# A gated mixer kernel: the front part in a written order, and sines taken once per matrix

## The chip, the cores and the metric

The kernel runs on one core of a Trainium2 chip. The metric is the device time of one execution in microseconds (us); the median of several runs counts. Engines are named as in the profile: PE multiplies matrices, DVE is the vector engine, ACT the scalar engine (activations and copies), POOL is GpSimd, and SP issues most of the loads. A DMA can also be issued from the queues of ACT and POOL.

## The reference

Everything is in bf16, with S = 2048 rows of D = 640 and F = 1536. From one input x (`A_q`) two branches are made and mixed by a gate:

```python
g = sigmoid((x * gate_w).sum(-1))
# branch A: a short convolution, then a long one by FFT
k_shift = sum over t<4 of shift(k, t) * shift_k[:, t]
kv = k_shift * v
y  = irfft(rfft(pad(kv)) * rfft(pad(ssm_k)))[:S] + kv * ssm_D
a  = x * y
# branch B: a mixer over shifted rows, then an MLP
h  = gelu(layernorm(x) @ w1)          # four column groups, shifted by 1, -1, 2, -2 rows
x1 = x + shifted(h) @ w2
b  = x1 + gelu(layernorm(x1) @ w3) @ w4
out = g * a + (1 - g) * b
```

## The kernel before

The 2048 rows are laid out as 128 partitions by 16 units `u` (`N2`), and four units make a chunk; `Q` holds x, one tile for each chunk.

**Branch B.** `norm_stats` (DVE, with `ve` and `rs` on POOL at L178 and L180) and `norm_apply` normalise a chunk: DVE writes `xn` (L308), PE transposes it (L315), ACT copies it to `XNT` (L90). `first_product` (PE L349) multiplies by w1 in three groups of columns: first the group of five matmuls whose left side is `W1E` (gathered columns of w1), then two groups of ten. ACT's gelus (L342) write the results to their shifted places in `GS`, those of the first group by way of `u4` and copies on POOL (L359). `second_product` (L427) multiplies a unit by w2 and DVE adds it to `Q` (L430). `third_product` (L441) and `fourth_product` (L454) are the MLP; they need `W3` and `W4`.

**Branch A.** The long convolution is a two-step Fourier transform by matrices. `filter_transpose` (L295) turns a loaded tile `HN` of the filter; DVE and ACT copy it to `HTA` and `HTB`. `step1` (L275, with ACT's copy to `AR` and a DMA to `SH` or `SX` in memory) does the first step, of the filter (`filt`, 32 rows of two matmuls) and of the convolved input. `short_conv` is eleven DVE instructions for each chunk (L413 to L418) and uses `CJ`, four copies on POOL from the loaded `CJR` (L388). `spectrum` does the second step with the matrix `M2`, multiplies, and goes back with `G1` and `G2`; `y_group` finishes.

**The matrices.** `F1`, `F1T`, `M2`, `G1` and `G2` are sines made on the chip. In `gen_step2`, POOL makes integer phases (`iota`, L244, L252, L256), DVE wraps them (L212), and ACT takes the sine (L215). `M2`, `G1` and `G2` consist of four blocks each, of which a partition needs one and holds zeros in the others. `masked_sines` takes the sine of 1024 phases four times for each matrix, with a scale and a bias per partition that are zero where the block is to be zero: twelve sines of 128x1024.

**Order.** The program is traced in the order in which it is written, and a scheduler then orders each engine's queue by that order and by when it expects operands; `tc.issue_after(x)` puts a block behind instruction x on its engine. `merge(a, b, ratio)` interleaves two generators by the costs that they yield. Tiles with one tag share a fixed number of buffers: `XNT` and `CJR` share two ("xnt"), all of PSUM's `pst` and `psw` tiles share two ("pm"), `GEN` (phases), `HTA`, `W3`, `W4` and others share three ("w"), and eleven serve `KT`, `VT`, `CJ`, `AR` and most others ("b5").

The core of the written order of the front is

```python
X0 = norm_apply(tiles_of(c4[0]), st0, "a")
...
filter_transpose(0)
st1 = norm_stats(tiles_of(c4[1]))
next(gen)
run(first_product(0, X0))
X1 = norm_apply(tiles_of(c4[1]), st1, "a")
filter_transpose(1)
```

and so on for chunks 2 and 3. `conv_front` then interleaves the convolution with `filt` and the mixer, and loads W4 (`load_w4`, on ACT's queue) behind the 32nd row of `filt`.

Of the kernel before, what the change touches and what calls it, by code (L numbers as in the profile page):

```python
# [10 lines left out]
ALU = mybir.AluOpType  # L11
# [6 lines left out]
def kernel(  # L18
# [68 lines left out]
    def evac(eng, o, i, scale=None):  # L87
        if eng == "a":
            if scale is None:
                nc.scalar.copy(out=o, in_=i)  # L90
            else:
                nc.scalar.activation(out=o, in_=i, func=ACT.Copy, scale=scale)  # L92
        else:
            assert scale is None
            nc.vector.tensor_copy(out=o, in_=i)
# [17 lines left out]
    def load_h(dt):  # L113
# [4 lines left out]
    load_q(0)  # L118
    W12 = weights("W12", [P, 2, DT, D])
# [3 lines left out]
    load_q(1)  # L123
    load_h(0)
    load_q(2)
    load_h(1)
# [3 lines left out]
    nc.scalar.copy(out=W1E.rearrange("p k (g r) -> p k g r", r=R),  # L130
                   in_=W1N.rearrange("p k (g c) -> p k g c", c=CG)[:, :, :, P:CG])
# [10 lines left out]

    IDB = consts.tile([P, P], BF16, name="IDB")
# [58 lines left out]
    with tc.issue_after(last_f.ins):  # L202
        st0 = norm_stats(tiles_of(range(4)))


# [5 lines left out]
    def masked_sines(dst, jj, ms, inner):  # L211
        nc.vector.tensor_scalar(out=jj, in0=jj, scalar1=TU - 1, scalar2=None, op0=ALU.bitwise_and)  # L212
        jv = jj.rearrange("p (o m n) -> p m o n", o=2, n=16)
        for j in range(4):
            nc.scalar.activation(out=dst[:, :, :, j, :] if inner else dst[:, :, j, :, :], in_=jv, func=ACT.Sin,  # L215
                                 bias=ms[:, 1, j:j + 1], scale=ms[:, 0, j:j + 1])

    midp = pbits(120, 0.125, 0, "midp")
    basep = pbits(3, 16, 1, "basep")
    basei = pbits(15, 512, 1, "basei")  # L220
    klf = pbits(3, 1, 0, "klf")
    kli = pbits(48, 0.0625, 0, "kli")
    offp = [pbits(4, -512, 6144 + 2048 * ro, f"offp{ro}") for ro in range(2)]
    offi = [pbits(64, -64, 6144 - 2048 * o, f"offi{o}") for o in range(2)]
    nc.vector.scalar_tensor_tensor(out=basei[:], in0=kli[:], scalar=16.0, in1=basei[:], op0=ALU.mult, op1=ALU.add)
# [3 lines left out]
    masks = []  # L229
    for name, kl in (("f", klf), ("i", kli)):  # L230
        ms = consts.tile([P, 2, 4], F32, name="ms" + name)
        for a, amp in ((0, 2 * PI_ / TU), (1, -PI_)):
            for j in range(4):
                nc.vector.tensor_scalar(out=ms[:, a, j:j + 1], in0=kl[:], scalar1=float(j), scalar2=amp,
                                                     op0=ALU.is_equal, op1=ALU.mult)
# [532 lines left out]
```

## Time and profile before

| what | value |
|---|---|
| median of 3 runs | 304.11 us (302.92 to 304.94) |
| profiled execution: time, span | 305.71 us, 303.9 us |
| PE busy, matmuls | 247.5 us, 1559 |
| DVE busy | 194.2 us |
| ACT busy | 189.0 us |
| POOL busy | 45.4 us |
| granted PE clock, mean | 0.955 |

The span runs from the first to the last instruction of the core; the execution's own time is a little longer. Busy times are sums over instructions; an engine's idle time costs nothing unless the end waits for it, so the waits and the order of the instructions have to be read beside the shares. In the views, `L123` is a line of the kernel, `xN` a number of instructions, and `A <- B` says that A waited for B.

### The profile page before, as it was taken

Reading aid. Unit: us, or ns where it says so; the run is one execution under the profiler, and the core shown is the slowest. Engines: PE = TensorE matmul, PEld = TensorE weight load, DVE = VectorE, ACT = ScalarE, POOL = GpSimd, SP = SyncE. Lnnn points to the kernel's source line nnn. Section 1 sums busy time; section 2 is a strip of 40 time slices with the busy share of each in tenths; the row PEclk is TensorE's granted clock in tenths of the full one; section 3 lists DMA queues with packets and bytes.
Section 4 is the critical chain, followed back from the end, with each engine's and each line's share of the span. In section 5 each row is a group of like instructions: output and inputs, shape, how many; then the busy total and the mean of one; then the engine's idle time right before and its main releaser. Section 6 shows DMA issues by size and latency. Waiting matters only on the chain.

```text
span 303.9 us, 4266 instructions
## 1 busy us (share of the span) xinstructions
PE 247.5 (81%) x1559; PEld 150.7 (50%) x1572; DVE 194.2 (64%) x411; ACT 189.0 (62%) x264; POOL 45.4 (15%) x79
## 2 busy tenths in 40 slices
PE   0257289389979965999999678999988997799994
PEld 0252255146545522676457455665545764445673
DVE  8781852407729869898918878996443465502982
ACT  1329975445885763743775436659789878646740
POOL 8734351620600300000000330000000000000000
PEclk9999679689999979899999999999999999799999
DMA  7991097002242599522556798696786654278741
GB/s 230 380 319 64 0 365 328 1 2 87 86 175 86 191 323 349 175 88 86 177 171 216 240 345 238 217 279 197 244 280 188 199 168 135 89 263 341 283 171 65
DMA packets 28087, 59.59 MB, mean 196 GB/s; under 512 B 2051, under 2 KB 19203, under 8 KB 28066
## 3 DMA queue, kind: packets, MB, share of 16 engines
q1 hardware_dynamic: 13042, 38.18, 38.2%
q10 hardware_dynamic: 14224, 17.70, 15.8%
q0 software_dynamic: 800, 3.44, 3.3%
q8 instruction: 12, 0.20, 0.3%
q14 instruction: 9, 0.07, 0.1%
HBM read 35.71 MB, written 18.35 MB: 178 GB/s over the span
## 4 chain that ended last, share of the span: by engine, by line
PE 58%; DMA 15%; ACT 12%; DVE 5%; POOL 4%; issue 2%; SPq 1%; ACTq 0%; POOLq 0%
PE psw L454 15%; PE psw L441 14%; PE psw L427 6%; DMA BX<-SX 5%; PE ps L275 5%; PE psz L517 5%; ACT XNT L90 4%; PE psw L349 4%; DMA HN<-in_A_ssm_k_dram 4%; DMA SH<-AR 4%; PE psy L578 3%; DMA CJR<-in_A_shift_k_dram 2%; PE psx L501 2%; PE psh L488 2%; DVE st L175 2%
## 5 line engine op out<-in xcount | busy, mean ns | idle before, releaser
L454 PE MATMUL psw<-W,G 128*128 128x320 bf16 x384 | 60.9, 299 | 2.4 <-ACT XNT L90 2.4
L90 ACT CAST AR<-ps 128x640 bf16<-128x640 f32 x64 | 41.6, 701 | 28.3 <-PE ps L275 24.3
L441 PE MATMUL psw<-XNT,W 128*128 128x512 bf16 x231 | 58.3, 387 | 0.8 <-ACT G L342 0.5
L454 PEld LDWEIGHTS <-G 128*128 128x128 bf16 x384 | 37.5, 98 | 17.5 <-issue 2.9
L506 DVE TENSOR_TENSOR XPB<-XPB,HS 128x640 bf16<-128x640 bf16 x64 | 28.3, 486 | 18.3 <-ACT XPB L90 18.3
L441 PEld LDWEIGHTS <-W 128*128 128x128 bf16 x240 | 23.7, 99 | 24.1 <-issue 2.0
L92 ACT ACTIVATE HS<-psh 128x640 bf16<-128x640 f32 x32 | 22.6, 713 | 18.4 <-PE psh L488 18.4
L342 ACT ACTIVATE G<-psw 128x1024 bf16<-128x1024 f32 x24 | 24.7, 1031 | 11.8 <-PE psw L441 11.7
L430 DVE TENSOR_TENSOR Q<-psw,Q 128x640 bf16<-128x640 f32 x16 | 12.9, 811 | 26.9 <-PE psw L427 26.9
L175 DVE BATCH_NORM_STATS2 st<-Q 128x6 f32<-128x320 bf16 x64 | 27.7, 469 | 0.5 <-DMA Q<-in_A_q_dram 0.3
L517 PE MATMUL psz<-XPB,G 128*128 128x320 bf16 x128 | 23.9, 310 | 4.9 <-DVE XPB L506 1.6
L427 PE MATMUL psw<-W,GS 128*128 128x320 bf16 x160 | 24.7, 299 | 3.3 <-ACT XNT L90 2.3
L349 PE MATMUL psw<-XNT,W 128*128 128x512 bf16 x80 | 23.5, 453 | 4.6 <-ACT u L342 4.6
L90 ACT CAST XPB<-psx 128x640 bf16<-128x640 f32 x32 | 22.3, 696 | 7.6 <-PE psx L501 7.4
L90 ACT COPY XNT<-pst 128x2048 bf16<-128x2048 bf16 (+1 forms) x16 | 19.1, 1241 | 12.2 <-PE pst L315 9.2
L308 DVE TENSOR_SCALAR xn<-Q,mv,rs 128x640 bf16<-128x640 bf16 x32 | 15.2, 520 | 15.6 <-PE pst L315 9.5
L295 PE MATMUL psh<-IDB,HN 128*128 128x128 bf16 x80 | 8.4, 278 | 18.4 <-DMA HN<-in_A_ssm_k_dram 14.8
L275 PEld LDWEIGHTS <-F 128*128 128x128 bf16 x128 | 12.5, 100 | 16.9 <-issue 8.3
L427 PEld LDWEIGHTS <-GS 128*128 128x128 bf16 x160 | 15.6, 98 | 10.0 <-issue 3.9
L178 POOL TENSOR_SCALAR ve<-mv 128x4 f32<-128x4 f32 x8 | 3.0, 370 | 111.6 <-DVE mv L176 111.6
L517 PEld LDWEIGHTS <-G 128*128 128x128 bf16 x128 | 12.6, 100 | 13.8 <-issue 5.7
L416 DVE TENSOR_TENSOR acc<-acc,tmp 128x2560 bf16<-128x2560 bf16 x12 | 17.9, 1488 | 0.3
(109 smaller groups left out, 359.8 us busy)
## 6 DMA issues: line engine op xcount, KB each, us to landing
SH<-AR ACTq DMA_DIRECT2D x8, 640.0 KB, 3.1
SX<-AR ACTq DMA_DIRECT2D x8, 640.0 KB, 3.3
BH<-SH SPq DMA_DIRECT2D x8, 640.0 KB, 4.2
HS<-HS SPq DMA_DIRECT2D x32, 160.0 KB, 2.9
BX<-SX SPq DMA_DIRECT2D x8, 640.0 KB, 5.5
SZ<-ZG ACTq DMA_DIRECT2D x8, 640.0 KB, 3.2
ZT<-SZ SPq DMA_DIRECT2D x8, 640.0 KB, 5.7
HN<-in_A_ssm_k_dram SPq DMA_DIRECT2D x5, 512.0 KB, 10.3
```

Source lines behind the costliest of these rows:

```text
L90: nc.scalar.copy(out=o, in_=i)
L92: nc.scalar.activation(out=o, in_=i, func=ACT.Copy, scale=scale)
L175: nc.vector.bn_stats(out=st[:, h, :], in_=src[i][:, h * HD:(h + 1) * HD])
L275: nc.tensor.matmul(ps[:, comp, 0:HD], lhsT=F1[:, comp, :], rhs=src[:, c0:c0 + HD], start=True, stop=True)
L342: nc.scalar.activation(out=o, in_=i, func=ACT.Gelu_apprx_tanh)
L349: nc.tensor.matmul(ps[:, j, :], lhsT=w1_cols(dt, nt), rhs=XNT[:, dt, :], start=(dt == 0), stop=(dt == DT - 1))
L416: nc.vector.tensor_tensor(out=acc[:], in0=acc[:], in1=tmp[:], op=ALU.add)
L427: nc.tensor.matmul(ps[:, h, 0:HD], lhsT=GS[:, nt, u, :], rhs=W2P[:, nt, h * HD:(h + 1) * HD], start=(nt == 0), stop=(nt == DT - 1))
L441: nc.tensor.matmul(ps[:, j, :], lhsT=W3[:, dt, (f + j) * P:(f + j + 1) * P], rhs=XNT[:, dt, :], start=(dt == 0), stop=(dt == DT - 1))
L454: nc.tensor.matmul(ps[:, h, 0:HD], lhsT=G[ft // 4][:, ft % 4, i * P:(i + 1) * P], rhs=W4[0][:, ft, h * HD:(h + 1) * HD], start=(ft == 0), ...
L506: nc.vector.tensor_tensor(out=xp[:, 1 + a, :], in0=xp[:, 0, :], in1=HS[t // 2][:, a, t % 2, :], op=ALU.mult)
L517: mm = nc.tensor.matmul(pz[:, h, 0:HD], lhsT=gm[:, t].rearrange("p a b c -> p (a b c)"), rhs=XP[t][:, 1 + a, h * HD:(h + 1) * HD], start=( ...
```

## The change

- Everything from the making of `IDB` to the end of the fourth `first_product` stands between `front.__enter__()` and `front.__exit__()`: PE, DVE, ACT and POOL run it in the order in which it is written. SP's queue isn't in that list.
- The loads of x's chunks are put ahead of the filter's: Q0, Q1, W1, Q2, HN0, Q3. W2, the second filter tile, the halo and the first K and V follow.
- The phases are mapped by six ACT instructions (`affine`) from the iotas; one DVE instruction makes the product `m1`. One sine for each matrix is written to block 3; `masked_blocks` later fills the four blocks from it under 0/1 masks, by DVE and ACT in turn, one for each step of the convolution of chunks 1 to 3.
- `W1E` is gathered by DVE (`gather_w1`) instead of ACT.
- Within `first_product(c)`, the next chunk's `norm_apply` and the statistics of the one after it are written between the second and the third group.
- `CJR`'s load and its split into `CJ` are apart. Two steps of the first convolution, and the whole of `second_product` for the first four units, lie in the front; none of `filt` does, and `conv_front` takes five rows of it for each remaining step of the first convolution instead of three.

```diff
     load_q(0)
+    load_q(1)
...
     nc.sync.dma_start(out=W1N, in_=B_w1.rearrange("(kt p) n -> p kt n", p=P))
-    load_q(1)
+    load_q(2)
     load_h(0)
-    load_q(2)
-    load_h(1)
+    load_q(3)
...
     W1E = edge("W1E")[:].rearrange("p (k n) -> p k n", n=P)
-    nc.scalar.copy(out=W1E.rearrange("p k (g r) -> p k g r", r=R),
-                   in_=W1N.rearrange("p k (g c) -> p k g c", c=CG)[:, :, :, P:CG])
+
+    def gather_w1():
+        nc.vector.tensor_copy(out=W1E.rearrange("p k (g r) -> p k g r", r=R),
+                              in_=W1N.rearrange("p k (g c) -> p k g c", c=CG)[:, :, :, P:CG])
...
+    ET = mybir.EngineType
+    front = tc.manual_schedule(engines={ET.PE, ET.DVE, ET.Activation, ET.Pool})
+    front.__enter__()
...
-    with tc.issue_after(last_f.ins):
-        st0 = norm_stats(tiles_of(range(4)))
...
-    def masked_sines(dst, jj, ms, inner):
-        nc.vector.tensor_scalar(out=jj, in0=jj, scalar1=TU - 1, scalar2=None, op0=ALU.bitwise_and)
-        jv = jj.rearrange("p (o m n) -> p m o n", o=2, n=16)
-        for j in range(4):
-            nc.scalar.activation(out=dst[:, :, :, j, :] if inner else dst[:, :, j, :, :], in_=jv, func=ACT.Sin,
-                                 bias=ms[:, 1, j:j + 1], scale=ms[:, 0, j:j + 1])
...
+    GA, GB, GC = GENW[:, 0, :], GENW[:, 1, :], GENW[:, 2, :]
+    icf, ick, icn, m1 = GA[:, 0:512], GA[:, 512:1024], GB[:, 0:512], GB[:, 512:1024].bitcast(F32)
...
     midp = pbits(120, 0.125, 0, "midp")
     basep = pbits(3, 16, 1, "basep")
...
-    masks = []
+    basei = pbits(15, 512, 1, "basei")
+    kli = pbits(48, 0.0625, 0, "kli")
+    nc.vector.scalar_tensor_tensor(out=basei[:], in0=kli[:], scalar=16.0, in1=basei[:], op0=ALU.mult, op1=ALU.add)
+    offi = [pbits(64, -64, 6144 - 2048 * o, f"offi{o}") for o in range(2)]
+    off2 = consts.tile([P, 1], F32, name="off2")
+    nc.vector.memset(off2[:], 6144.0)
...
+    def affine(o, i, scale, bias):
+        nc.scalar.activation(out=o, in_=i, func=ACT.Identity, scale=scale, bias=bias)
+
+    def wrap(jj):
+        nc.vector.tensor_scalar(out=jj, in0=jj, scalar1=TU - 1, scalar2=None, op0=ALU.bitwise_and)
+
+    def block(dst, inner, j):
+        return dst[:, :, :, j, :] if inner else dst[:, :, j, :, :]
+
+    def sines(dst, jj, inner):
+        nc.scalar.activation(out=block(dst, inner, 3), in_=jj.rearrange("p (o m n) -> p m o n", o=2, n=16),
+                             func=ACT.Sin, bias=NPI[:], scale=2 * PI_ / TU)
+
+    for ro in range(2):
+        affine(GC[:, 512 * ro:512 * ro + 512], icf, midp[:], offp[ro][:])
+    st0 = norm_stats(tiles_of(range(4)))
+    nc.vector.scalar_tensor_tensor(out=m1, in0=ick, scalar=basei[:], in1=icn, op0=ALU.add, op1=ALU.mult)
+    wrap(GC)
+    for o in range(2):
+        affine(GA[:, 512 * o:512 * o + 512], m1, 1.0, offi[o][:])
+    sines(M2, GC, True)
+    for o in range(2):
+        affine(GC[:, 512 * o:512 * o + 512], m1, 1.0, (0.0, off2[:])[o])
+    klf = pbits(3, 1, 0, "klf")
+    MK = []
...
+        mk = consts.tile([P, 4], F32, name="mk" + name)
+        MK.append(mk)
...
+    def masks():
+        for mk, kl in zip(MK, (klf, kli)):
...
-                nc.vector.tensor_scalar(out=ms[:, a, j:j + 1], in0=kl[:], scalar1=float(j), scalar2=amp,
...
-    def gen_step2():
-        GA, GB, GC = GENW[:, 0, :], GENW[:, 1, :], GENW[:, 2, :]
...
-        for ro in range(2):
-            nc.gpsimd.tensor_scalar(out=GC[:, 512 * ro:512 * ro + 512], in0=icf, scalar1=midp[:],
-                                    scalar2=offp[ro][:], op0=ALU.mult, op1=ALU.add)
-        masked_sines(M2, GC, masks[0], True)
-        yield 0.0
...
-        nc.gpsimd.tensor_scalar(out=m1, in0=ick, scalar1=basei[:], scalar2=None, op0=ALU.add)
-        nc.vector.tensor_tensor(out=m1, in0=m1, in1=icn, op=ALU.mult)
-        for (dst, jj, offs) in ((G1, GA, (offi[0][:], offi[1][:])), (G2, GC, (0.0, 6144.0))):
-            for o in range(2):
-                nc.gpsimd.tensor_scalar(out=jj[:, 512 * o:512 * o + 512], in0=m1, scalar1=offs[o], scalar2=None,
-                                        op0=ALU.add)
-            masked_sines(dst, jj, masks[1], False)
-            yield 0.0
+                nc.vector.tensor_scalar(out=mk[:, j:j + 1], in0=kl[:], scalar1=float(j), scalar2=None,
...
+                                        op0=ALU.is_equal)
+
+    def masked_blocks():
+        n = 0
+        for dst, mk, inner in ((M2, MK[0], True), (G1, MK[1], False), (G2, MK[1], False)):
+            for j in range(4):
+                if n % 2:
+                    with tc.issue_after(held["a"].ins):
+                        nc.scalar.activation(out=block(dst, inner, j), in_=block(dst, inner, 3), func=ACT.Copy,
+                                             scale=mk[:, j:j + 1])
+                else:
+                    with tc.issue_after(held["v"].ins):
+                        nc.vector.tensor_scalar(out=block(dst, inner, j), in0=block(dst, inner, 3),
+                                                scalar1=mk[:, j:j + 1], scalar2=None, op0=ALU.mult)
+                n += 1
+                yield 0.0
...
+        held["v"] = evac("v", HTA[0][:, :, dt * P:(dt + 1) * P], pst[:, 0:12, :])
+        held["a"] = evac("a", HT[3][:, :, dt * P:(dt + 1) * P], pst[:, 12:16, :])
...
-    def load_cj():
+    def load_cjr():
         cjr = main.tile([P, D, 4], BF16, name="CJR", tag="xnt", bufs=2)
         nc.gpsimd.dma_start(out=cjr[:], in_=A_shift_k.partition_broadcast(P))
+        return cjr
+
+    def split_cj(cjr):
         cj = big("CJ")
         for j in range(4):
             nc.gpsimd.tensor_copy(out=cj[:, j, :], in_=cjr[:, :, j])
...
     def load_halo(t):
+        nc.gpsimd.memset(t[0:1, :, :], 0.0)
         nc.sync.dma_start(out=t[1:113, :, :], in_=kv_[0:112, N2 - 3:N2, :])
...
+        blocks = masked_blocks()
         for g in range(NG):
             if 1 < g + 1 < NG:
                 load_kv(g + 1)
-            for c_ in short_conv(g):
+            for c_ in (short_conv(g) if g else conv0):
                 yield c_
-                for _ in range(3):
+                for _ in range(3 if g else 5):
                     next(rows, None)
+                if g > 0:
+                    next(blocks, None)
             if g == 0:
                 rows = chain(rows, step1(xrows(0), SX, 0))
             else:
                 run(rows)
                 if g < NG - 1:
                     rows = step1(xrows(g), SX, g)
+        run(blocks)
...
-    gen = gen_step2()
     X0 = norm_apply(tiles_of(c4[0]), st0, "a")
-    next(gen)
+    gather_w1()
+    wrap(GA)
+    wrap(GC)
+    sines(G1, GA, False)
+    sines(G2, GC, False)
     gs_edges()
+    st1 = norm_stats(tiles_of(c4[1]))
+    load_w2()
+    load_h(1)
     KHALO = big("KHALO", [P, 3, D])
-    nc.gpsimd.memset(KHALO[0:1, :, :], 0.0)
-    next(gen)
-    load_w2()
+    load_halo(KHALO)
+    load_kv(0)
     load_h(2)
-    load_q(3)
-    filter_transpose(0)
-    st1 = norm_stats(tiles_of(c4[1]))
-    next(gen)
-    run(first_product(0, X0))
+    first = first_product(0, X0)
+    next(first)
+    next(first)
+    masks()
     X1 = norm_apply(tiles_of(c4[1]), st1, "a")
-    filter_transpose(1)
+    st2 = norm_stats(tiles_of(c4[2]))
+    run(first)
     DROW = row("DROW")
     nc.gpsimd.dma_start(out=DROW[0:1, :], in_=A_ssm_D.rearrange("(a d) -> a d", a=1))
-    CJ = load_cj()
+    CJR = load_cjr()
+    filter_transpose(0)
     load_h(3)
-    load_halo(KHALO)
-    load_kv(0)
+    first = first_product(1, X1)
+    next(first)
+    next(first)
+    X2 = norm_apply(tiles_of(c4[2]), st2, "a")
+    st3 = norm_stats(tiles_of(c4[3]))
+    run(first)
+    filter_transpose(1)
     load_h(4)
-    st2 = norm_stats(tiles_of(c4[2]))
-    run(first_product(1, X1))
-    filter_transpose(2)
-    X2 = norm_apply(tiles_of(c4[2]), st2, "a")
-    load_kv(1)
     W3 = weights("W3", [P, DT, Fh])
     nc.sync.dma_start(out=W3[:], in_=B_w3.rearrange("(kt p) f -> p kt f", p=P))
+    load_kv(1)
+    CJ = split_cj(CJR)
+    second = second_product(US[0])
+    next(second)
+    next(second)
+    first = first_product(2, X2)
+    next(first)
+    next(first)
+    X3 = norm_apply(tiles_of(c4[3]), st3, "a")
+    run(second)
+    run(first)
+    sy0 = norm_stats(tiles_of(US[0]))
     nc.gpsimd.dma_start(out=GWB[:], in_=gate_w.partition_broadcast(P))
-    st3 = norm_stats(tiles_of(c4[3]))
+    conv0 = short_conv(0)
+    filter_transpose(2)
+    next(conv0)
     filter_transpose(3)
-    run(first_product(2, X2))
+    first = first_product(3, X3)
+    next(first)
+    next(first)
+    next(conv0)
     filter_transpose(4)
-    X3 = norm_apply(tiles_of(c4[3]), st3, "a")
+    run(first)
+    front.__exit__(None, None, None)
     rows = chain(filt(), load_w4())
-    merge(second_product(US[0]), rows, 0.4)
-    sy0 = norm_stats(tiles_of(US[0]))
-    merge(first_product(3, X3), rows, 0.4)
     Y0 = norm_apply(tiles_of(US[0]), sy0, "a")
```

## The prediction

> **What bounds the kernel now.** I read the page first (engine shares, the 40 slices), then the table of stretches, then the waits of the front alone, then the timeline of its instructions.
>
> The page, its engine line and the slice row of PE:
>
> ```profile
> PE 247.5 (81%) x1559; PEld 150.7 (50%) x1572; DVE 194.2 (64%) x411; ACT 189.0 (62%) x264; POOL 45.4 (15%) x79
> ...
> PE   0257289389979965999999678999988997799994
> ```
>
> A slice is 7.6 us. PE idles 56.4 us of the span, and most of that in the first nine slices; behind them it is 85 to 90% busy. So the kernel is a badly filled front and a PE-bound rest. The table of stretches (columns: PE, PEld, DVE, ACT, POOL busy; clock; DMA share; GB/s) says it in numbers:
>
> ```profile
> 0.00:82.30 82.30, 51.10 (x321) 30.56 (x326) 45.00 (x147) 48.22 (x64) 37.76 (x69) 0.90 0.48 172
> 82.30:303.90 221.60, 196.35 (x1240) 120.13 (x1247) 149.16 (x266) 140.79 (x200) 7.67 (x11) 0.98 0.61 205
> 82.30:107.80 25.50, 21.89 (x139) 12.81 (x139) 17.79 (x29) 17.89 (x27) 2.90 (x3) 1.00 0.44 147
> ```
>
> 82.3 us is where the last of the four `first_product` calls ends on PE, which is also where the written order of the new front ends. PE idles 31.2 us before it and 25.2 us behind it. The waits of the stretch 0 to 66 us name the holes:
>
> ```profile
> ...
> PE psh L295 <- DMA HN<-in_A_ssm_k_dram: 14.8, 2, 13.1
> ...
> ACT XNT L90 <- PE pst L315: 8.1, 1, 8.1
> ...
> PE psw L349 <- ACT XNT L90: 6.2, 2, 4.4
> ...
> PE psw L349 <- ACT u L342: 4.6, 1, 4.6
> ...
> ACT XNT L90 <- POOL CJ L388: 3.1, 1, 3.1
> ```
>
> First, PE's queue holds the filter's transposes (L295) ahead of x's, and waits until 13.07 and 16.69 us for the filter to land, though x's `xn` had been ready since 11.9; so x's first `XNT` starts at 20.69. Second, `u`'s gelu is stuck behind the sines, in this timeline:
>
> ```profile
> 22.93 4.64 ACT L215 ACTIVATE M<-GEN,msf 128x1024 bf16<-128x1024 int32 x4
> ...
> 32.46 4.65 ACT L215 ACTIVATE G<-GEN,msi 128x1024 bf16<-128x1024 int32 x4
> ...
> 52.60 3.05 POOL L388 COPY CJ<-CJR 128x640 bf16<-128x640 bf16 x4 [4.13 <-DMA CJR<-in_A_shift_k_dram]
> ...
> 55.67 2.35 ACT L90 COPY XNT<-pst 128x2048 bf16<-128x2048 bf16 x2 [3.07 <-POOL CJ L388]
> ```
>
> ACT is full from 22.9 to 37.1 with twelve sines (13.9 us), and PE, but for one filter transpose, stands from 29 until the gelus start at 38.4. Third, the last two rows: `CJR` shares the two buffers of `XNT`, so chunk 2's `XNT` waits until POOL has copied `CJ`, and PE stands 4.36 us behind it.
>
> **The change, worked along the path.** Each step is the later of what it waits for, plus durations from rows of before.
>
> *Statistics.* On DVE some 20 one-column instructions now stand ahead of the first `bn_stats`. Such rows lie 0.06 apart when independent and take 0.14 each when each needs the last: 1.2 to 2.8 us. They are written in dependent pairs, so 2.8: statistics start at 3.5 + 2.8 = 6.3 (before 3.8), take four times 0.87 to 9.8, then `ve`, `rs` 1.4 to 11.2. The phase product (a 128x512 row of 0.69) and one wrap (0.70) lie under `rs`. The four `xn` (0.45 each) run 11.4 to 13.2, begun 2.0 later than before.
>
> *Phases and sines.* Six affine maps leave POOL (rows of 0.8 to 1.6) for ACT. No row is an integer map on ACT; the nearest are the 128x512 copies at 0.61 and half a sine at 0.62, and the full 128x1024 sine row of 1.24 is the upper end. At 0.62 the first four and M2's sine (1.16) end before x's transposes do, and the last two maps lie under those transposes: nothing on the path. At 1.24 the path is 2.0 later. Two more sines follow `XNT`. Twelve sines become three: 10.4 us of ACT gone.
>
> *Chunk 0.* With x first, PE transposes from 11.9 to 13.8 (the wait for the filter is gone), ACT copies `XNT` 1.88 + 0.5 to 16.6 against 23.0 before. W1 now lands behind Q1, by the 11.3 us at which before had both; the gather (0.44 to 0.72, now on DVE) ends at 13.7. Fifteen matmuls follow, 0.43 cold and 0.22 warm, to 21.9; the sines and one table load (1.28) end at 20.3, so `u` hardly waits. Chunk 1's statistics and `xn` are done by 21.8 (its `ve` stands behind 1.8 us of edge memsets on POOL, long done; the 1.69 us KHALO memset now stands ahead of `u`'s POOL copies, which are read 20 us later). Transposes 1.3, `XNT` 1.88, and, since PSUM's two "pm" buffers hold the transposes, the last ten matmuls start only then, at 24.9: chunk 0 ends at 27.1 (before 42.9).
>
> *The stall that stays.* The filter's 16 transposes (1.06) and fifteen matmuls of chunk 1 bring PE to 31.4, chunk 2's transposes to 32.7. Its `XNT` needs a buffer. Chunk 1's is still read by ten matmuls written behind, which need the PSUM that this `XNT` frees; so only `CJR`'s is left. `CJR` can be loaded from 27.5 (x's first `XNT` free, behind DROW's issue on POOL), and lands, by before's 7.3, at 35.5; no other row of that transfer exists, the bounds are 2.0 (DROW's small one) and 14.1 (the slowest VT load). On POOL `split_cj` stands behind chunk 3's `ve`, `rs`, done at 35.9. So it runs 35.9 to 38.9, `XNT` to 40.9, and PE idles 8.2 us where before it idled 4.4. Slow landing costs up to 6.4 more; a fast one gains nothing.
>
> Behind its 4.36 us gap before's matmuls run 0.43 apart for 5 us (57.6 to 62.7) until they fall to 0.22; the new gap is charged the same way below.
>
> The Trainium skill speaks against this transfer's place ("SBUF — State Buffer", Summary: rules for kernel authors): descriptors for a load on POOL's queue are starved while DVE runs in its fast modes, and no run here shows it. If chunk 2's `xn` (1.8) held the transfer back for as long, `split_cj` would start 1.4 later and the sum be 1.4 worse.
>
> *From 40.9.* Ten matmuls 4.05 (warming), filter 1.06, two units of `second_product` 2.72, fifteen matmuls 3.24, transposes 1.33, wait for `XNT` 1.75, two units 2.72, ten matmuls 2.16, filter 2 x 1.06, fifteen 3.24, filter 1.06, ten 2.16: 27.6, so 68.5. Where the slow clock lasts longer the same sum gives 70.0. I take **69.3**.
>
> *The ledger at that point.* Before stands there at 82.3, but its PE has already done 4.9 us of the filter's `step1` (L275) and ACT twelve of its evacuations; the new front has done none. PE's lead is 82.3 - 4.9 - 69.3 = **8.1 us**.
>
> *What the rest pays.* ACT now owes 12 x 0.70 = 8.4 us of evacuations, and six masked copies at 1.03 to 1.24 (the 128x1024 rows), of which about half early, 3.1. In the stretch 82.3 to 107.8 ACT was busy 17.9 of 25.5; it becomes 17.9 + 8.4 + 3.1 = 29.4, while PE's 21.9 + 4.9 at before's rate of 86% would need 31.2. ACT would have to be 94% busy. If its waits vanish because its queue is full: no loss. If it keeps its old 70%: 42.0, a loss of 10.8. I take a third, **3.6**, since PE has ten microseconds of `second_product` ready to bring forward. On DVE six masked copies (0.43 by the `xn` row to 0.95 by the HTA row) cost 2.6 to 5.7 and two steps of the first convolution (1.33, 0.90, 0.81, 0.82, 1.48) moved into the front save 5.3: nought, under PE.
>
> The skill speaks against the masked copies on ACT ("ScalarE: Activation LUTs", Rules for kernel authors: multiplications belong on VectorE, up to three times faster in bf16); no row here has that copy on both engines. With all twelve on DVE that loss would be a third of 37.6 less 31.2, and the sum 1.5 better.
>
> Loads: SP keeps its own order; HN0, W2 and the filter land by 15 to 26 us and are first read at 27 and 45; KV0 is read at 63. W3 needs the buffer that the sines free, now at 19 instead of 37, and is read after 80. GWB's load moves behind POOL's last `rs` of the front and is read in the spectrum. All free.
>
> **Sum.** 303.9 - 8.1 + 3.6 = 299.4 of span, that is 4.5 less. The profiled execution took 305.71, 1.6 above the runs' median of 304.11, with 1.8 outside the span; I take the difference from the median: **299.6**. A measurement of this kernel tells about 1% from no change.
>
> **Rivals.**
> *(a) The stall goes too* (chunk 2's `XNT` finds a buffer without `CJ`): PE saves the 8.2, the front ends at 61.1, the lead is 16.3: 303.9 - 16.3 + 3.6 = 291.2. For it: only which buffer is given; against it: the row of before in which exactly this `XNT` waits for exactly this copy. Chance 0.14.
> *(b) ACT becomes the bound behind the front* (slower). W4's load is issued on ACT's queue behind the 32nd row of the filter. From 69.3 ACT must do `XNT` 2.4, 32 rows 22.4, masks 3.1, gelus 6.2: 34.1 us, or 48.7 at its 70%, so W4 lands (11.1) at 114.5 or 129. PE reaches `fourth_product` after 1.3 + 9.5 + 5.4 + 13.0 = 29.2 at 87%, at 102.9; with 10.8 brought forward, 113.7. The wait is 0.8 to 15.3; from 8.1 on the kernel is slower, and at the top it takes 303.9 - 8.1 + 15.3 = 311.1 (311.3 for the median). For it: all the filter's evacuations now come at once; against it: ACT has idle time in every later slice. Chance 0.25.
> *(c) The gain is lost to contention*: `CJR` lands late (6.4) and the ACT loss stays: 303.9 - 8.1 + 3.6 + 6.4 = 305.8, or 302.6 with half of it; no measurable change. For it: at 28 to 36 us the loads of chunk 3's filter rows, W3 and the second K and V may be under way; against it: `rs` holds `split_cj` as long as before's 7.3 would. Chance 0.17.
> *(d) The sines aren't saved*: the profile would show twelve Sin rows; the diff leaves three, so I give it nothing.
>
> **How the numbers follow.** The forecast, 295 to 301, has 0.44; with (a) faster has 0.58, within 1% 0.17 from (c), slower 0.25. The range runs from 290, just under (a), to 310, just under the top of (b); the forecast's own range is 294 to 305.
>
> **What would show it.** Right: `XNT` of chunk 0 at 14 to 17 us; three large Sin rows; chunk 2's `XNT` waiting for `CJ` at about 39; `first_product`'s last row (before L349) at 68 to 71; VT's first product near 80 instead of 107.8; ACT over 90% for 25 us behind it. Wrong: the front ending beyond 76, or PE waiting for W4, or no wait for `CJ`.

## The result, and the profile after

The changed kernel took 315.0 us in the median of four runs (312.9 to 317.1), the kernel before 303.7 in the same comparison: ratio 1.037, 95% interval 1.028 to 1.046. It is slower, where 299.6 had been forecast. The profiled execution took 313.56 us with a span of 311.8, so its span is 7.9 longer than that of before; the median is 11.3 longer. Ratios here and below are to the kernel before on the same chip, and leave disturbed executions out (the profiled one of cjr_own is such a one), so they can differ a little from the quotient of two medians.

The page of the changed kernel, PE's busy share and slices:

```profile
PE 246.6 (79%) x1572; PEld 148.1 (48%) x1572; DVE 198.5 (64%) x411; ACT 186.7 (60%) x265; POOL 38.1 (12%) x72
...
PE   0266729795986972899999883999998997599994
...
PEclk9997969999996998699999997899999999999999
```

PE idles 65.2 us of the span, 8.8 more than before. New holes stand behind the front: the thirteenth slice (94 to 101 us) and above all the sixteenth (117 to 125). The granted clock is low there, or in the slice that follows.

The table of stretches (PE, PEld, DVE, ACT, POOL busy; clock; DMA share; GB/s), and then the waits from 73 to 140 us:

```profile
0.00:73.00 73.00, 43.61 (x304) 25.73 (x304) 48.12 (x140) 32.34 (x46) 30.07 (x59) 0.93 0.52 176
...
73.00:100.00 27.00, 19.93 (x124) 11.31 (x121) 22.04 (x40) 21.91 (x32) 3.10 (x6) 0.92 0.43 147
...
119.00:126.00 7.00, 0.55 (x3) 0.22 (x3) 0.00 (x0) 2.93 (x3) 0.00 (x0) 0.77 1.05 380
```

```profile
DVE acc L438 <- DMA SH<-AR: 17.2, 1, 17.2
...
PE psw L479 <- DMA W<-in_B_w_dram: 6.4, 1, 6.4
...
PE ps L295 <- ACT AR L90: 6.3, 16, 2.4
DVE tmp L438 <- ACT AR L90: 3.7, 1, 3.7
ACT AR L90 <- DVE tmp L438: 2.8, 1, 2.8
```

(In the changed kernel L295 is `step1`, L370 `first_product`, L438 to L443 `short_conv`, L479 `fourth_product`.) The front now ends at 73, with 29.4 us of PE idle in it. From 119 to 126 PE works 0.55 us and DVE not at all. The timeline of that place (start, duration, engine, line) shows how it comes about:

```profile
114.16 0.33 SPq L425 DMA_DIRECT2D KT<-in_A_k_dram  x1
114.17 0.44 ACTq L659 DMA_DIRECT2D W<-in_B_w_dram  x1
...
114.88 0.59 ACTq L300 DMA_DIRECT2D SH<-AR  x1
...
119.00 1.45 ACTq L300 DMA_DIRECT2D SX<-AR  x1
...
125.88 4.30 PE L479 MATMUL psw<-W,G 128*128 128x320 bf16 x17 [6.43 <-DMA W<-in_B_w_dram]
127.62 1.16 DVE L438 TENSOR_TENSOR acc<-KT,CJ 128x1920 bf16<-128x1920 bf16 x1 [17.17 <-DMA SH<-AR]
```

W4's load (1.9 MB) leaves at 114.17, behind the 32nd filter row, 7.2 us later than before (106.96), and takes 11.67 to land. The last SH write of 640 KB, issued 0.7 us after it, takes 12.6 us, where the median SH write takes 4.2; two loads of K and V (the first line) are on their way at the same time. Its AR is the buffer that the third convolution needs: DVE stands until 127.62. And PE, whose queue is in order, stands at the first matmul of `fourth_product`, with the next rows of `step1` behind it.

### The profile page after: what moved, and what is told of

Same layout as the page of the kernel before. It is cut to its first block, busy times and chain, and to the rows that moved or that the text cites. A ratio compares the mean times of both kernels' runs of the same rounds, so it can differ in the third digit from the quotient of the medians.

```text
span 311.8 us, 4270 instructions
## 1 busy us (share of the span) xinstructions
PE 246.6 (79%) x1572; PEld 148.1 (48%) x1572; DVE 198.5 (64%) x411; ACT 186.7 (60%) x265; POOL 38.1 (12%) x72
## 4 chain that ended last, share of the span: by engine, by line
PE 53%; DVE 22%; DMA 10%; ACT 8%; POOL 3%; issue 3%; SPq 0%; ACTq 0%; POOLq 0%; DVEq 0%
PE psw L479 16%; PE psw L466 14%; DVE st L178 5%; PE psz L542 5%; DMA W<-in_B_w_dram 4%; PE psw L452 4%; DMA BX<-SX 4%; PE psw L370 3%; ACT XNT L90 3%; PE psy L603 3%; PE ps L295 3%; PE psx L526 2%; DVE acc L441 2%; DVE tmp L439 2%; PE psh L513 2%
## 5 line engine op out<-in xcount | busy, mean ns | idle before, releaser
L479 PE MATMUL psw<-W,G 128*128 128x320 bf16 x384 | 64.7, 308 | 8.3 <-DMA W<-in_B_w_dram 6.4
L466 PE MATMUL psw<-XNT,W 128*128 128x512 bf16 x240 | 60.6, 387 | 0.2 <-ACT G L363 0.2
L479 PEld LDWEIGHTS <-G 128*128 128x128 bf16 x384 | 38.6, 101 | 25.2 <-DMA W<-in_B_w_dram 6.8
L466 PEld LDWEIGHTS <-W 128*128 128x128 bf16 x240 | 23.9, 99 | 24.0 <-issue 2.2
L370 PE MATMUL psw<-XNT,W 128*128 128x512 bf16 x80 | 21.7, 425 | 10.5 <-ACT XNT L90 9.6
L336 PE MATMUL pst<-IDB,xn 128*128 128x128 bf16 x160 | 13.6, 231 | 18.2 <-POOL GS L348 13.8
L452 PE MATMUL psw<-W,GS 128*128 128x320 bf16 x160 | 23.8, 299 | 4.1 <-ACT XNT L90 2.9
L295 PEld LDWEIGHTS <-F 128*128 128x128 bf16 x128 | 12.5, 98 | 19.4 <-issue 12.5
L336 PEld LDWEIGHTS <-xn 128*128 128x128 bf16 x160 | 11.0, 103 | 21.6 <-DVE xn L329 17.8
L452 PEld LDWEIGHTS <-GS 128*128 128x128 bf16 x160 | 15.6, 98 | 10.8 <-issue 4.8
L370 PEld LDWEIGHTS <-W 128*128 128x128 bf16 x80 | 8.7, 108 | 22.0 <-issue 15.2
L526 PE MATMUL psx<-BX,M 128*128 128x320 bf16 x64 | 14.5, 308 | 5.8 <-DMA BX<-SX 4.9
L542 PEld LDWEIGHTS <-G 128*128 128x128 bf16 x128 | 12.4, 98 | 13.8 <-issue 6.9
```

The source lines that it names most:

```text
L295: nc.tensor.matmul(ps[:, comp, 0:HD], lhsT=F1[:, comp, :], rhs=src[:, c0:c0 + HD], start=True, stop=True)
L336: nc.tensor.transpose(out=pst[:, dd, i * P:(i + 1) * P], in_=xns[i][:, (d0 + dd) * P:(d0 + dd + 1) * P], identity=IDB[:])
L370: nc.tensor.matmul(ps[:, j, :], lhsT=w1_cols(dt, nt), rhs=XNT[:, dt, :], start=(dt == 0), stop=(dt == DT - 1))
L452: nc.tensor.matmul(ps[:, h, 0:HD], lhsT=GS[:, nt, u, :], rhs=W2P[:, nt, h * HD:(h + 1) * HD], start=(nt == 0), stop=(nt == DT - 1))
L466: nc.tensor.matmul(ps[:, j, :], lhsT=W3[:, dt, (f + j) * P:(f + j + 1) * P], rhs=XNT[:, dt, :], start=(dt == 0), stop=(dt == DT - 1))
L479: nc.tensor.matmul(ps[:, h, 0:HD], lhsT=G[ft // 4][:, ft % 4, i * P:(i + 1) * P], rhs=W4[0][:, ft, h * HD:(h + 1) * HD], start=(ft == 0), ...
```

## The experiments

The theory: the filter's 32 rows, which now all come behind the front, meet a convolution that has been moved ahead of them and holds the "b5" buffers that AR needs; so W4's load, which is behind the rows, leaves late, and nothing covers it. The rival is the prediction's own: ACT's work behind the front is the bound.

The runs in one table. PE idle is the span less PE's busy time, of the profiled execution; "front end" is the end of the last `first_product`.

| kernel | median us | ratio (95%) | PE idle us | front end | W4 issued | clock |
|---|---|---|---|---|---|---|
| before (its profile) | 303.7 | 1 | 56.4 | 82.4 | 107.0 | 0.955 |
| after_again | 314.6 | 1.038 (1.034 to 1.041) | 63.3 | 73.5 | 115.4 | 0.933 |
| w4_24_sp | 303.7 | 0.999 (0.995 to 1.003) | 55.9 | 73.1 | 107.1 | 0.959 |
| b5_12 | 300.4 | 0.988 (0.982 to 0.993) | 54.8 | 74.3 | 104.6 | 0.971 |
| kv2_late | 303.4 | 0.999 (0.996 to 1.001) | 57.9 | 72.4 | 100.8 | 0.977 |
| w4_after_sh | 310.3 | 1.024 (1.021 to 1.027) | 60.6 | 73.4 | 116.2 | 0.955 |
| filt_early | 307.1 | 1.012 (1.007 to 1.018) | 59.0 | 74.6 | 99.0 | 0.961 |
| before_filt_late | 307.9 | 1.013 (1.008 to 1.017) | 57.8 | 77.5 | 111.4 | 0.936 |
| before_w4_24_sp | 303.4 | 0.999 (0.996 to 1.003) | 56.8 | 80.9 | 97.1 | 0.959 |
| cjr_own | 306.2 | 1.001 (0.996 to 1.006) | 59.0 | 65.3 | 106.0 | 0.948 |
| w4_24_masks_dve | 302.0 | 0.992 (0.989 to 0.995) | 57.5 | 73.9 | 106.1 | 0.977 |
| best3 | 292.9 | 0.968 (0.965 to 0.971) | 49.1 | 63.6 | 97.0 | 0.992 |
| best1 | 291.6 | 0.958 (0.953 to 0.963) | 47.9 | 66.0 | 96.2 | 0.988 |
| best2 | 295.7 | 0.971 (0.967 to 0.976) | 49.7 | 65.7 | 99.8 | 0.977 |
| before_own_w4 | 298.7 | 0.979 (0.975 to 0.984) | 54.6 | 76.3 | 92.5 | 0.971 |

**The changed kernel again** (after_again), as the reference on another chip.

> The changed kernel as it is, as the reference for the others of this call: 313 to 317 if its loss belongs to the kernel; if the 315 was partly a lower clock on the chip that it ran on, 306 to 311.

314.6 us: the loss belongs to the kernel. Its clock of 0.933 is low too; the section on the hardware shows, for the first profile of this kernel, that the clock falls where PE stands.

**W4's load earlier** (w4_24_sp).

```diff
             yield from step1(hrows(g), SH, g)
+            if g == 2:
+                yield from load_w4()
...
-        nc.scalar.dma_start(out=W4[0][:], ...
+        nc.sync.dma_start(out=W4[0][:], ...
...
-    rows = chain(filt(), load_w4())
+    rows = filt()
```

> The changed kernel with one edit: W4's load is asked for after the 24th of the 32 filter rows (when HTA's twelve slices have been used) and is issued from SP, not from ScalarE behind the 32nd. The theory: behind the front the 32 filter rows of `step1` come in one lump, with few "b5" buffers left for AR, so W4's load, which stands behind them, leaves at 114.2 and lands at 125.8, and PE waits 6.4 us for it ahead of the first `fourth_product`. By it the load leaves near 107.5, lands near 119, the 6.4 us go from 6.4 to under 1, and the time falls by 4 to 6 us, to 309 to 311. The rival, ScalarE as the bound behind the front (the copies of `step1`, the gelus and the masked copies add up to more than fits): W4 comes earlier but the wait is put on by another row, 314 to 316. A second rival, that the early load takes DMA time from KT2, VT2 and the SH writes: 315 to 318.

The load left at 107.13, as expected, and PE's wait for it is gone from the list. The size was missed: 3.9 points of the ratio, some 11.7 us, instead of 4 to 6. The first `fourth_product` starts only 1.1 earlier (124.74), so the 6.4 us were not the whole. What moved with it is the convolution: conv 2 starts at 122.55 instead of 127.62, its product VT2 comes at 135.4 instead of 143.0, and the second SX write, which had been queued behind PE's wait, leaves at 120.2 instead of 131.9.

**The SH write ahead of W4** (w4_after_sh), to part the late buffer from the wait for W4.

```diff
-            nc.scalar.dma_start(out=bass.AP(tensor=dst_dram.tensor, ...
+            wr["last"] = nc.scalar.dma_start(out=bass.AP(tensor=dst_dram.tensor, ...
...
-        nc.scalar.dma_start(out=W4[0][:], ...
+        with tc.issue_after(wr["last"].ins):
+            nc.scalar.dma_start(out=W4[0][:], ...
```

> The changed kernel, W4's load still behind the 32nd filter row and still from ScalarE, but held until the eighth SH write has been issued. In the changed kernel W4's load leaves at 114.17 and the last SH write at 114.88, behind it; that write lands 12.6 us later instead of 3.6, and conv 2, which needs its buffer, stands 17.2 us, to 127.6. The theory that this stand of the convolution is what costs the time, and PE's 6.4 us wait for W4 little of it: conv 2 starts near 119 to 121, W4 lands 1 us later than before (127), and the time falls by 5 to 9 us, to 306 to 310. The rival, that the wait for W4 itself costs the time: 314 to 317, though conv 2 starts early.

Conv 2 started at 121.4, near what was expected, but only 1.3 points (4 us) came back; neither view had the size right. Two lines of its waits say why:

```profile
DVE acc L439 <- DMA SH<-AR: 10.6, 1, 10.6
...
DVE tmp L439 <- DMA SX<-AR: 7.0, 1, 7.0
```

With the load still on its way, the next writes of AR are the late ones: `tmp` now waits 7.0 us for an SX write, and VT2 comes at 140.8. So the early SH write is worth about a third; that the rest is the load's own lateness follows from w4_24_sp, where the load is early and all comes back.

**One more buffer** (b5_12). Twelve "b5" buffers; room for it is made by three "e" buffers and one shared integer scratch tile.

```diff
-        ... name=name, tag="b5", bufs=11)
+        ... name=name, tag="b5", bufs=12)
...
-        ... name=name, tag="e", bufs=4)
+        ... name=name, tag="e", bufs=3)
...
-        ti = consts.tile([P, 1], I32, name=name + "i")
+        ti = consts.tile([P, 1], I32, name="pbi", tag="pbi")
```

> The changed kernel with 12 instead of 11 "b5" buffers (paid for by three "e" buffers instead of four and one shared integer scratch tile for the small phase constants). The theory that the two "b5" buffers left for AR hold the filter rows back: with three, ScalarE's copies no longer wait for SH's writes at 96.3, the 24 first rows are out by 103 to 105 instead of 107.4, W4's load leaves by 110 instead of 114.2, conv 2's first row no longer waits 17.2 us for an SH write; the time falls by 4 to 8 us, to 307 to 311. The rival, ScalarE's own work as the bound: its rows stand as close as before, 314 to 316. A third view, that the rows' order on PE holds them (one group of rows after each step of the convolution), gives 313 to 316 too, but with the waits for SH gone from the list of waits.

300.4 us, 5.0 points better than the changed kernel: more than expected. W4's load stands where it stood in the program, and leaves at 104.6 instead of 114.2, because the rows ahead of it no longer wait and because the scheduler now puts it ahead of the sixth SH write on ACT's queue, not behind the seventh. ACT's work is the same (187.1 us).

**K and V of the third group later** (kv2_late). It takes no work away, only a load that holds two buffers from 86 us on.

```diff
-            if 1 < g + 1 < NG:
-                load_kv(g + 1)
+            if g == 2:
+                load_kv(3)
...
                 run(rows)
+                if g == 1:
+                    load_kv(2)
```

> The changed kernel with one edit: KT2 and VT2 are asked for behind the 32nd filter row, where conv 1 has given its buffers back, not ahead of conv 1. Two more "b5" buffers are then free for AR from 86 us on, and no load of K and V stands before W4's. By the theory of the buffers ScalarE's and PE's waits around AR between 90 and 105 go, the sixth SH write leaves at 99 to 103 instead of 107.4 and W4's load by 110, landing by 118; conv 2 then waits for KT2 (10 to 12 us of landing) until 121 to 124 instead of 127.6: 303 to 309. If the rows' place in the order and not the buffers holds W4's load: 312 to 316.

303.4 us, 3.9 points back, with the sixth SH write at 101.5 and W4's load at 100.77. Of the changed kernel first, then of this one, the stretches 94 to 98 and 98 to 102:

```profile
94.00:98.00 4.00, 1.45 (x7) 0.70 (x6) 1.96 (x4) 1.89 (x4) 0.00 (x0) 0.69 0.53 200
98.00:102.00 4.00, 3.76 (x11) 1.31 (x9) 2.30 (x3) 2.60 (x4) 0.00 (x0) 0.50 0.60 221
```

```profile
94.00:98.00 4.00, 3.16 (x16) 1.45 (x15) 3.97 (x5) 4.00 (x7) 0.00 (x0) 1.00 0.48 174
98.00:102.00 4.00, 4.00 (x22) 2.06 (x21) 3.90 (x5) 3.88 (x6) 0.00 (x0) 1.00 0.46 163
```

In the changed kernel DVE and ACT are half idle here, and PE too in the first stretch: a ring of AR, SH write and `tmp`, each waiting for a buffer of the other. With two buffers free, ACT (fourth column of busy times) is full, and the time falls by 11 us. So ACT at its limit is not what cost the time.

The idle stretch itself isn't either. In w4_24_sp, which took 303.7, it stands as before:

```profile
94.00:98.00 4.00, 1.65 (x8) 0.70 (x6) 2.11 (x4) 2.10 (x4) 0.00 (x0) 0.82 0.59 220
98.00:102.00 4.00, 3.54 (x10) 1.32 (x10) 2.36 (x3) 2.54 (x4) 0.00 (x0) 0.50 0.60 221
```

What w4_24_sp, b5_12 and kv2_late have in common is that W4's load leaves as soon as the 24th filter row is through PE (at 107.1, 104.5 and 100.7); in the changed kernel that row was through at 106.6, and the load left 7.6 us later, behind the seventh SH write. So the ring by itself cost little; it cost time as far as it held W4's load back. In b5_12 and kv2_late the scheduler moved the load as well, so they don't show what the buffers are worth by themselves.

**Rows back into the front** (filt_early).

```diff
-    first = first_product(3, X3)
-    next(first)
-    next(first)
-    next(conv0)
     filter_transpose(4)
-    run(first)
+    next(conv0)
     front.__exit__(None, None, None)
     rows = chain(filt(), load_w4())
+    merge(first_product(3, X3), rows, 0.8)
```

> The changed kernel with its written order ended ahead of chunk 3's first product, all filter transposes ahead of it, and filter rows of `step1` begun within that product (0.8 us of rows per us of product, about 11 rows), as the kernel before begins them within its second and fourth front products. The theory that the 32 rows in one lump behind the front cost the time: the 24th row is out 3 to 6 us earlier than 107.4, W4 leaves by 110, the time falls by 3 to 6 us, to 309 to 312. The rival, PE's and ScalarE's sum of work as the bound behind 73 us: the rows are only moved into a front that is already full, 314 to 316. Against both: chunk 3's product waits behind filter transposes 3 and 4, whose HN tiles land late; then the front ends 2 to 4 us later and the time stays or rises, 315 to 318.

307.1 us, 2.5 points back, 7.6 us, a little more than the theory's 3 to 6. W4's load left at 99.0, far earlier than needed, but the eighth SH write only at 112.9, and the first `fourth_product` came at 129.3; which of these holds the rest was not tried.

**The same in the kernel before** (before_filt_late).

```diff
-    merge(second_product(US[0]), rows, 0.4)
+    run(second_product(US[0]))
...
-    merge(first_product(3, X3), rows, 0.4)
+    run(first_product(3, X3))
```

> The kernel before with one edit: no filter rows of `step1` within its second and fourth front products; all 32 come behind the fourth `first_product`, as in the changed kernel. If it is the missing rows in the front alone that bring the loss (W4's load later, both stands behind it), this kernel loses as the changed one did: the front ends some 3 to 5 us earlier, W4's load leaves at 112 to 116 instead of 107, and the time is 309 to 316. If the rows only cost where the convolution has also been moved ahead of them (before, conv 1 runs until 121.9 and covers W4 and the SH write), the time is 302 to 306.

307.9 us, between the two views: a loss of 1.3 points, a third of the changed kernel's. The front ends 4.9 us earlier. But the reading that the edit leaves the convolution in its place was wrong: without the rows the scheduler moves it up too (VT1 at 111.7 instead of 121.9, KT2 asked for at 85.0 instead of 102.7), and the same waits appear, 4.6 us of PE for W4 and 5.0 of DVE for an SH write. So this run can't tell rows from convolution. kv2_late shows that the convolution's early loads are needed for the loss, filt_early that the rows' place is, too.

**W4 earlier in the kernel before** (before_w4_24_sp): the edit of w4_24_sp.

> The kernel before with the edit that took 11 us off the changed one: W4's load behind the 24th filter row, issued from SP. The theory that only the change made W4's place matter (before, conv 1 runs from 108.8 to 121.9 and covers both the late SH write and W4): no difference, within 1% of the kernel before, 302 to 305. The rival, that W4's early load is a gain of its own in any order: 295 to 300.

No difference. Before, the last SH write was late as well; one line of its chain of waits:

```profile
107.68 12.05 DMA SH<-AR
```

But conv 1 ran until VT1 at 121.93 and used the buffers that it had, and PE reached `fourth_product` at 125.18, after W4 had landed. The same late write was there, but other work ran meanwhile.

**CJR in its own buffer** (cjr_own).

```diff
-        cjr = main.tile([P, D, 4], BF16, name="CJR", tag="xnt", bufs=2)
+        cjr = big("CJR", [P, D, 4])
```

> The changed kernel with one edit: CJR has a "b5" buffer of its own and no longer one of the two that XNT uses, so chunk 2's XNT does not wait for POOL's split of CJR. Every theory expects PE's 7.9 us wait at 37 to 45 gone and the front's last `first_product` row 5 to 8 us earlier, at 65 to 68 instead of 73. If the rest simply follows the front (what is lost behind it is a fixed cost), the time falls by the same 5 to 8 us, to 307 to 310. If the rest is held by something that does not move with the front (CJ, which is split at 40.3 to 43.1 whatever the order; the loads of HN and W3; the buffers, with one fewer until the split), less than 2 us come through, 313 to 315.

The front's last row moved from 73.5 to 65.3, and 8 us or more came through (8.4 us by the medians, 3.6 points or 11 us by the ratios). That is the prediction's rival (a), with its price, at another place on the scale. PE's wait for W4 stayed (6.98 us), so this loss is apart from the other.

**All copies under masks on DVE** (w4_24_masks_dve), on top of w4_24_sp.

```diff
-                if n % 2:
+                if False:
```

> The changed kernel with W4's load behind the 24th row (303.7 us) and all twelve masked copies on DVE (0.45 us each there) instead of six on ScalarE (1.16 each). If ScalarE were the bound behind the front, the 7 us taken off it would bring 2 to 6 us, 298 to 302; the prediction's estimate was 1.5 us, 302.2. If ScalarE's time is not the bound: 303 to 305, since DVE gets 2.7 us more.

302.0 us, ratio 0.992 against 0.999: some 2 us, with intervals that lie just apart. A copy takes 0.47 us on DVE and 1.16 on ACT. This is at the edge of the first view (298 to 302), so here ACT's work behind the front may have cost those 2 us; best2 below, with the same edit on another kernel, went the other way.

**The edits together** (best3 = cjr_own and w4_24_sp; best1 = that and b5_12; best2 = that and the masks on DVE; before_own_w4 = the two edits of best3 in the kernel before).

> The changed kernel with CJR in a buffer of its own and W4's load behind the 24th filter row, issued from SP. If the two losses are independent (7.9 us of PE waiting for chunk 2's XNT in the front; W4 and the SH write behind it), the time is the 303.7 of the one edit less the 6 to 8 us by which the other moved the front's end: 296 to 299. If both edits recover the same lost time (the fuller filter part then waits for W3, HN or the buffers instead), 301 to 304.

> The kernel that took 292.9 us (changed kernel, CJR in its own buffer, W4 behind the 24th row) with 12 "b5" buffers as well. There conv 2 still stands 11.1 us for an SH write's buffer, until 112.4, which holds DVE and not PE. If that stand is covered by PE's own queue: 291 to 294. If the spectrum's first reads follow the last SX write, as they seem to in the runs so far (last SX write issued at 148.6, 142 us ahead of the end): conv 2 starts 4 to 5 us earlier and the time falls to 288 to 290.

> The three edits together (CJR in its own buffer, W4 behind the 24th row from SP, 12 "b5" buffers) with all twelve masked copies on DVE: the same as without the last edit, within 1.5 us, if ScalarE isn't the bound; 2 to 5 us less if it is.

> The kernel before with both edits of the kernel that took 292.9 us: CJR in a "b5" buffer of its own, W4's load behind the 24th filter row from SP. It shows what the change itself is worth once both obstacles are gone on both sides. In the kernel before PE stands 4.4 us behind the XNT that waits for CJ, in the changed one 7.9. By the theory that the new front is a gain of its own, which only the two collisions hid, this kernel gains 3 to 6 us at most, to 297 to 300, and the change is worth 4 to 7 us on top. The rival, that the two edits alone bring it all: 291 to 295.

best3 took 292.9 us, below the range expected: the two losses are independent (7.0 points together, 3.6 and 3.9 alone), and without both holes the clock is 0.992. best1 is inside the first view's 291 to 294 by its median, and a point (3 us) below best3 by the ratios, so between the two views; conv 2 started 3.5 earlier, but the last SX write left only 0.7 earlier (147.9). best2, with the masks on DVE, is 1.3 points worse than best1, which neither view allowed: there ten of the twelve copies stand on DVE at 83 to 92 us, among the convolution's rows, and the sixth SH write goes from 97.0 to 100.5. That the one led to the other was not tried. before_own_w4 took 298.7, inside its 297 to 300: the edits help the kernel before by 2.1 points, and the change is worth 1.2 points, 3.5 us, on top of them (0.4 to 1.9 points by the ends of the intervals), a little less than the 4 to 7 us expected. best1 beats both kernels: 0.958 (0.953 to 0.963). Its page shows what is gone, and what PE still idles, mostly at the start:

```profile
PE 242.4 (84%) x1572; PEld 146.1 (50%) x1572; DVE 198.1 (68%) x411; ACT 186.6 (64%) x265; POOL 38.5 (13%) x72
...
PE   0075978885986976899979899899998996999994
...
PEclk9999899999999999999999999999999999799999
```

## Why the prediction was wrong, step by step

**Statistics, phases, chunk 0: right in order, some 4 us late.** `bn_stats` began at 6.77 (6.3 forecast), the four tiles were 0.99 apart and not 0.87, and `xn` began at 13.30, not 11.4. XNT began at 15.73, inside the forecast's 14 to 17, and ended 1.5 late. Chunk 0 ended at 31.3 instead of 27.1. One term of that: chunk 1's `xn`, from the timeline,

```profile
21.75 1.69 POOL L419 MEMSET KHALO<- 1x1920 bf16 x1
21.83 3.33 DVE L329 TENSOR_SCALAR xn<-Q,mv,rs 128x640 bf16<-128x640 bf16 x4 [1.12 <-POOL rs L183]
```

took 0.83 us each and not 0.45. Three sines were left, as the step said.

**The stall that stays: right.** `split_cj` stood behind chunk 3's `rs` and ran from 40.33 (forecast 35.9); PE idled 7.90 (forecast 8.2):

```profile
40.33 2.80 POOL L412 COPY CJ<-CJR 128x640 bf16<-128x640 bf16 x4
43.16 2.35 ACT L90 COPY XNT<-pst 128x2048 bf16<-128x2048 bf16 x2 [6.42 <-POOL CJ L412]
45.07 1.44 PE L370 MATMUL psw<-XNT,W 128*128 128x512 bf16 x3 [7.90 <-ACT XNT L90]
```

Of the wait the prediction named the engine, the tile and the reason. CJR's load took 4.6 us in this trace, 7.3 before, and 8.4 in the second profile of the same kernel (after_again). No run here shows whether its descriptors were starved, as the Trainium skill has it ("SBUF — State Buffer", Summary: rules for kernel authors); here `split_cj` waited for `rs` and not for the load. cjr_own shows that removing the stall is worth 8 us or more.

**From 40.9 and the ledger: the method right, the size off.** The stretch of 28.4 us measured 27.9; the front ended at 72.95 instead of 69.3, the 4.2 late that chunk 0 had brought less 0.5. The 4.9 us of `step1` that the ledger took off is what before_filt_late shows. The lead was 82.4 - 4.9 - 72.95 = 4.5 us and not 8.1.

**What the rest pays: the step that failed.** It charged 3.6 us, with bounds of 0 and 10.8, as a share of ACT's added work, and "Loads" closed with "All free". The rest paid 4.5 + 7.9 = 12.4 us by the spans, 4.5 + 11.3 = 15.8 by the medians. Where PE has no wait for W4, 3.6 was fair. In the pair with W4 earlier the lead is 80.9 - 4.9 - 73.1 = 2.9 and the net gain 0: the rest paid 2.9. In the pair best3 and before_own_w4 it is 76.3 - 4.9 - 63.6 = 7.8 for a net gain of 3.5: the rest paid 4.3. The other 11 us or so, which w4_24_sp brings back, are a term that the sum did not have: W4's load leaves late, and PE and the convolution stand for it and for the write behind it. The list of loads left out KT2 and VT2, which the earlier convolution asks for at 86 us instead of 102.7, and the step counted what ACT owes and not how many "b5" buffers the rows and the convolution share. The forecast sign "ACT over 90% for 25 us" failed accordingly: ACT was busy 21.9 of 27 us, 81%, behind the front.

**Rival (b) was the case, by another cause.** It put W4 behind the 32nd row, let it land at 114.5 to 129 and PE wait 0.8 to 15.3; W4 landed at 125.8 and PE waited 6.4. Of the three signs named as wrong, "PE waiting for W4" is the one that came. But its price counted ACT's time and PE's wait alone. With the measured lead, the forecast's 3.6 and the wait, 303.9 - 4.5 + 3.6 + 6.4 = 309.4, against a span of 311.8. One wait that this sum lacks stands much later, for a read of SX:

```profile
193.53 0.71 PE L526 MATMUL psx<-BX,M 128*128 128x320 bf16 x2 [4.91 <-DMA BX<-SX]
```

It is 3.60 us in after_again and 4.48 in cjr_own, the other two profiles in which PE waits over 6 us for W4, and at most 2.0 in every other profile. Why it comes is not shown. Runs without the wait for W4 recover more than 6.4: in w4_24_sp the rows behind it in PE's queue move too (the second SX write by 11.7 us), and this later wait falls to 1.29. The share of each is not known.

**VT's first product** ended at 90.1 (before 107.8) and not near 80. DVE was full from 73 to 90 us (17.0 of 17), with statistics, filter copies and sums for Q ahead of the convolution's rows: "On DVE nought, under PE" held for the end but not for that sign.

**The masked copies.** The skill's rule that the prediction weighed ("ScalarE: Activation LUTs", Rules for kernel authors) fits the rows, 0.47 against 1.16 us, and the 1.5 us that it would have brought measured about 2 in one kernel; in the other, a loss of some 4.

## What to carry to other kernels

When a change moves one stream of work ahead of another, count the buffers that both draw from a shared pool and every load that the earlier stream now asks for sooner, beside the engines' busy time; a ring of waits can leave all engines half idle, and here it cost time by the load that it held back. A large load that sits behind a row count in an in-order queue is only harmless while some other work is still running when it lands, so look at what covers it before and whether that cover stays. Two of the edits here, another buffer for CJR and W4's load ahead of the last eight rows, turned a loss of 3.7% into a gain of 3.2%.

## What the runs showed of the hardware

**Work behind a long stop of PE runs at half clock.** The table of stretches of the changed kernel, around its two long stops:

```profile
38.00:41.00 3.00, 0.00 (x0) 0.00 (x0) 0.78 (x3) 0.00 (x0) 1.92 (x3) 0.98 1.00 401
41.00:44.00 3.00, 0.00 (x0) 0.00 (x0) 0.00 (x0) 0.84 (x1) 2.12 (x4) 0.50 1.03 415
44.00:47.00 3.00, 1.93 (x5) 0.69 (x5) 0.00 (x0) 1.51 (x2) 0.00 (x0) 0.50 0.34 138
47.00:50.00 3.00, 3.00 (x26) 2.01 (x25) 0.29 (x1) 1.08 (x2) 0.00 (x0) 0.88 0.00 0
...
123.00:127.00 4.00, 1.12 (x5) 0.66 (x6) 0.00 (x0) 0.00 (x0) 0.00 (x0) 0.50 1.05 371
127.00:131.00 4.00, 4.00 (x22) 2.46 (x21) 3.12 (x4) 0.38 (x1) 0.00 (x0) 0.67 0.23 86
```

PE stood from 37.2 and from 119.5. By these rows the granted clock fell to 0.50 some 3.7 and 3.3 us into the stop, and stayed there for the first 2.6 and 3.8 us of work that followed. The length of a stop isn't all: the clock also fell at 27.2 and 95.5, in gaps of 1.7 and 2.4 us behind thin work. The same 1572 matmuls kept PE busy for 246.6 us in the changed kernel, with five such dips, and 241.9 in best3, with one: 4.7 us, 1.5% of the span. The clock gate of the Trainium skill ("TensorE: Matmul & The Clock Gate", Part 1: The HAM clock gate) gives a half clock after an idle window of about 3.4 us, and a full one after a busy window of about the same length; the two long stops agree with it. It puts the penalty of the ramp below 1% of a typical span; here, with several stops, the difference is 1.5%.

**A write behind a large load.** The SH write of 640 KB issued 0.7 us behind W4's 1920 KB load took 12.6 us, in before 12.0; the quickest of the eight took 3.2. The DMA engines were full meanwhile, at 380 GB/s, with loads of K and V among the traffic. In kv2_late and b5_12, where no load of K or V was issued in the 10 us before (in kv2_late one was issued 4.7 us later), the SH write behind W4 took 11.2 and 10.5.

**Vector rows beside POOL.** The four `xn` above took 3.33 us instead of 1.8 while POOL ran a memset and copies. No run here parts that from other causes.
